# Differences of the normalised rows made inside the third gate/up, in the rows' own buffer, and projection steps begun two blocks later

## The chip, the cores and the metric

The kernel runs on one core of a Trainium2 chip. The metric is the device time of one execution in microseconds (us); lower is better. Of the core's engines the text calls TensorE PE (its weight loads PEld), VectorE DVE, ScalarE ACT, GpSimd POOL and SyncE SP. SP issues the DMA transfers.

## What is computed

The reference, cut to what matters:

```python
xn = layernorm(x)                                  # x: 2048 rows x 512
q  = (xn @ wq) in 32 heads of 128
p  = softmax(q @ k_cache^T * 128**-0.5)            # 2048 cached keys a head
s  = (p @ v_cache, heads side by side) @ wo
g  = silu((relu(xn @ W_gate) * (xn @ W_up)) @ W_down)   # inner width 1792
out = x + s * g
```

All inputs and the output are bf16. Two branches, attention and a gated MLP, read the same normalised rows xn.

## The kernel before, in words

**Layout.** The 2048 rows are four row blocks Q of 512 (QB = 4). x_sb holds the rows, xn_sb the normalised rows (16 tiles of 128 rows), and xnT their transposes, 128 x 4 x 2048: the model width in four chunks of 128, the rows along the free dimension. Rows are normalised on POOL (`ln_norm`) and transposed from xn_sb to xnT by DMA from SP's queue (L457). Nothing reads xn_sb after that.

**MLP stage.** For each Q, `emit_gate_up(Q)` makes 14 feature tiles fc. One tile is four gate and four up matmuls on PE (L539, L543), a relu on ACT (L498) and the product hT on DVE (L504). `emit_down(Q)` multiplies by W_down into ps_acc (L562), ACT takes a tanh (L570), DVE makes g_sb (L582). Q = 0 works on centred rows of its own; the other three on xnT. "Third gate/up" is Q = 2.

**The PSUM ring.** ps_r is a ring of three slots of two banks. `ring_acquire` makes PE wait for whatever last emptied the slot. Gate/up pairs, score pairs, projection steps and output tiles all take slots from it, in the order in which they are written.

**Attention stage.** There are 128 blocks b: head h = b // 4, row block Q = b % 4. A block is eight pairs p of key tiles. For a pair PE makes two score matmuls into a ring slot (`emit_S_tile`, L806), ACT takes the exponential into PT (L818), and three pairs later (LAG = 3) PE multiplies with V (`emit_PV_tile`, L915). When a block's last pair is done, DVE takes the reciprocal of the sums (L835), scales into Onorm (L838), and SP issues a DMA transpose into OT_store (L843).

**Queries.** Heads 0 and 1 are projected with four plain matmuls per head and row block (`emit_qp`, L645), evicted by a DVE cast (L652). From head 2 on, two heads (a pair pr) share a scheme of seven products in place of eight: `emit_st(pr, c, step)` with c = 0, 1 and step = 0 to 3. Steps 0 to 2 are two products of two matmuls each, step 3 one product (L717); DVE combines the results into QT_sb through cu and cv (L722, L729). The products need sums over xnT, TX (four arrays of 128 x 2 x 1024, fp16), made once on DVE by `emit_tx` (L667 to L672), and sums over the weights, SW, made per pair on POOL by `emit_sw` (L681 to L694). Step 0 does not read TX; step 1 is the first that does and waits for its token on PE.

**The output.** `emit_oproj_tile` multiplies a finished group g of four heads by W_o for one row tile n (L761) and adds to s_acc on DVE. For n = 0 it waits for all transposes of the group (`t_toks`). `emit_final_tile` does the last group (L949).

**The order around the change** is written out by hand. After the last gate/up come the projections of head 0, three score pairs, the last `emit_down`, then `emit_tx` on DVE's queue and `emit_sw(1)` on POOL's, then the loop over pairs. A `plan` says which extra items PE does in block b at pair p (always in one visit `emit_M`, which takes one ring slot): in blocks 0 and 1 at pair 4 the projections of head 1; in blocks 0 to 119 at pair 0 one step, eight steps a pair; from block 17 to 123 one output tile a block, at pair 4, or in the visit of step 3, or at pair 0 where there is no step. In block 2 of each eight SP issues the load of the weights of the pair after next (L271) and POOL's sums of it are written. `SB_` buffers live in a stack that is closed after the MLP stage, and the buffers of attention (SW, s_acc, OT_store, Onorm, cu, cv and, before, TX) are laid over it.

Of the kernel before, what the change touches and what calls it, by code (L numbers as in the profile page):

```python
# [30 lines left out]
def _wait(eng, tok):  # L31
    if tok is None:
        return
    sem, val = tok
    if val <= 0:
        return
    eng.wait_ge(sem.h, val)


def _wait_all(eng, toks):  # L40
    best = {}
    for t in toks:
        if t is None:
            continue
        sem, val = t
        k = id(sem)
        if k not in best or best[k][1] < val:
            best[k] = (sem, val)
    for sem, val in best.values():
        _wait(eng, (sem, val))  # L50


def bass_recurrent_scan__mha_block_cached__glu_gated_reglu__prompt_kernel(
# [56 lines left out]
    with ExitStack() as es:  # L110
        _cnt = [0]

        def S_(shape, dt, name):
            _cnt[0] += 1
            return es.enter_context(nc.sbuf_tensor(f"{name}_{_cnt[0]}", shape, dt))
# [20 lines left out]
        Wq_sb = [S_([128, DC, 2, Dh], BF16, "Wq_sb") for _ in range(2)]  # L136
        Wo_sb = [S_([128, G, D], BF16, "Wo_sb") for _ in range(2)]
        PT = [S_([128, 2, NQ], BF16, "PT") for _ in range(NPB)]
        es_b = ExitStack()

        def SB_(shape, dt, name):
            _cnt[0] += 1
            return es_b.enter_context(nc.sbuf_tensor(f"{name}_{_cnt[0]}", shape, dt))

        xn_sb = SB_([128, NT, D], BF16, "xn_sb")
        xc_sb = SB_([128, 4, D], BF16, "xc_sb")
        xcT = SB_([128, DC, NQ], BF16, "xcT")
        r2 = SB_([128, 4, 1], F32, "r2")
# [312 lines left out]
        def ln_task(i):  # L461
# [12 lines left out]
            elif i == 4 * (QB - 1) + 1:  # L474
# [4 lines left out]
                ln_hold["r2"] = sem_ln3.sig(  # L479
                    dve.tensor_scalar(r2h[:], r2[:], 0.5, None, op0=ALU.mult))  # L480

        gr_free = [None] * NSLOT
        y_bank_free = [None, None]
        sig_free = [None, None]
# [30 lines left out]
        def emit_gate_up(Q):  # L515
            qs = slice(Q * NQ, (Q + 1) * NQ)
            h_tok = None
            for fc in range(FC):
                fs = slice(fc * 128, (fc + 1) * 128)
                if Q == 0 and fc < HFC:  # L520
                    s = half_slots[fc]
                    finish_gate_up(Q, fc, s, half_tok[(fc, 0)], half_tok[(fc, 1)])
                    continue
                if Q == 0 and fc == HFC:
                    s = None
                    _wait_all(pe, acc_free)
                else:
                    s = ring_acquire()
                g_ps, u_ps = gu_banks(s)
                if fc == 0:  # L530
                    _wait_all(pe, xt_ready[Q])
                xT, xs = (xcT, slice(0, NQ)) if Q == 0 else (xnT, qs)
                if Q == 0 and fc in FCS:
                    k = FCS.index(fc)
                    pe.wait_ge(sem_wg[k].h, 16)
                    pe.wait_ge(sem_wu[k].h, 16)
                ins = None
                for c in range(DC):
                    ins = pe.matmul(g_ps, Wg_sb[:, c, fs], xT[:, c, xs],  # L539
                                    start=(c == 0), stop=(c == DC - 1))  # L540
                gtok = sem_gate.sig(ins)
                for c in range(DC):
                    ins = pe.matmul(u_ps, Wu_sb[:, c, fs], xT[:, c, xs],  # L543
                                    start=(c == 0), stop=(c == DC - 1))
                gu_tok = sem_gu.sig(ins)
                h_tok = finish_gate_up(Q, fc, s, gtok, gu_tok)
            return h_tok

        def emit_down(Q, h_last_tok):
# [50 lines left out]
        Onorm = [S_([128, 4, Dh], BF16, "Onorm") for _ in range(NON)]  # L600
        OT_store = [S_([128, G, S], BF16, "OT_store") for _ in range(2)]
        fin_tmp = [S_([128, D], BF16, "fin_tmp") for _ in range(4)]
        TX = S_([128, 4, DC // 2, S // 2], F16, "TX")
        SW = [S_([128, 4, DC // 2, Dh], F16, "SW") for _ in range(2)]
        cu = S_([128, NQ], F32, "cu")
        cv = S_([128, NQ], F32, "cv")
# [46 lines left out]
            qt_ready[(h, Q)] = etok  # L653
            return etok

        HS = S // 2
        HC = DC // 2
        tx_tok = []
        sw_tok = {}

        def emit_tx():
            b11 = xnT[:, 0:HC, 0:HS]
            b12 = xnT[:, 0:HC, HS:S]
            b21 = xnT[:, HC:DC, 0:HS]
            b22 = xnT[:, HC:DC, HS:S]
            _wait_all(dve, [t for Q in range(QB) for t in xt_ready[Q]])
            t1 = sem_T.sig(dve.tensor_tensor(TX[:, 0], b12, b11, ALU.subtract))  # L667
            sem_T.sig(dve.tensor_tensor(TX[:, 2], b22, b12, ALU.subtract))  # L668
            _wait(dve, t1)
            t2 = sem_T.sig(dve.tensor_tensor(TX[:, 1], b22, TX[:, 0], ALU.subtract))  # L670
            _wait(dve, t2)
            tx_tok.append(sem_T.sig(dve.tensor_tensor(TX[:, 3], TX[:, 1], b21, ALU.subtract)))  # L672

        def emit_sw(pr):
            b = pr % 2
# [22 lines left out]
        def emit_st(pr, c, step, *banks):  # L698
# [33 lines left out]
            if step == 1:  # L732
                if c == 0:
                    _wait(pe, sw_tok[(pr, 1)])
                    _wait(pe, tx_tok[0])
                p6 = prod(6, banks[0])
                p5 = prod(5, banks[1])
                st_tok["u"] = comb(cu[:], cu[:], banks[0], waits=(p6, st_tok["u"]))
                st_tok["v"] = comb(cv[:], cu[:], banks[1], waits=(p5, st_tok["u"]))
                return [st_tok["v"]]  # L740
# [241 lines left out]
        def at(b, p, *items):  # L982
            plan.setdefault((b, p), []).append(list(items))

        at(0, 4, (emit_qp, 1, 1, 0), (emit_qp, 1, 1, 1))
        at(1, 4, (emit_qp, 1, 1, 2), (emit_qp, 1, 1, 3))
        GB = G * QB
        LB = NBLK - QB
        tiles = {}
# [8 lines left out]
                        at(LB + k // 4, 4 * (k // 2 % 2))  # L998
                    plan[(LB + k // 4, 4 * (k // 2 % 2))][-1].append((emit_oproj_tile, 1, g, n))
        for b in range(LB):  # L1000
            pr, r = b // 8 + 1, b % 8
            c, step = r // 4, r % 4
            t = tiles.pop(b, None)
            if pr < NPR:
                if step < 3:
                    at(b, 0, (emit_st, 2, pr, c, step))
                else:
                    at(b, 0, (emit_st, 1, pr, c, step), *([t] if t else []))
                    t = None
            if t:  # L1010
                at(b, 4 if pr < NPR else 0, t)
        assert not tiles
        for Q in range(QB - 2):
            for j in range(4):
# [10 lines left out]
            emit_S_tile(gp, 1)  # L1025
        emit_down(QB - 1, hlast)
        glu_done_tok = sem_g.cur()
        _wait(dve, glu_done_tok)
        emit_tx()
        emit_sw(1)  # L1030

        for gp in range(LAG, TOTP):
            gq = gp - LAG
            bq, hq, Qq, pq = blk_of(gq)
            items = plan.pop((bq, pq), None)
            b, h, Q, p = blk_of(gp)
            if p == 0 and Q == 0:
                sp_head_start(h)
            open_S_pair(gp)
            emit_S_tile(gp, 0)  # L1040
            if pq == 0 and bq % 8 == 2:
                pr = bq // 8 + 2
                if pr < NPR:
                    _wait(sp, qp_done_tok[pr - 2])
                    issue_wq(pr)
                    emit_sw(pr)
            if items:
                emit_S_tile(gp, 1)
                for it in items:
                    emit_M(it)  # L1050
            emit_PV_tile(gq, 0)
            if not items:
                emit_S_tile(gp, 1)
            emit_PV_tile(gq, 1)
# [42 lines left out]
```

## Time and profile before

| what | before |
|---|---|
| time, median of 3 runs (lowest to highest) | 1280.52 us (1280.49 to 1281.59) |
| the profiled execution, its own time | 1280.7 us |
| its span, first to last instruction | 1279.4 us |
| mean granted PE clock over the span | 0.997 |
| HBM read, written | 32.77 MB, 2.10 MB |
| share of the 16 DMA engines in the main queue (q1) | 27.8% |
| score exponentials (ACT L818) | 1024, 960.9 us busy |
| PV matmuls (PE L915) | 8192, 764.3 us busy |

The profile is of one execution. Its rows give, for an engine and a line of the kernel, the number of instructions, the time in which at least one of them ran, the mean length of one, and the idle time of the engine just ahead of them with what ended it. Matmuls overlap in the pipeline, so the length of one is not what it adds to the time. "The chain that ended last" follows the work back from the last instruction to what released each step. The granted clock is the share of full speed that PE was allowed.

### The profile page before, as it was taken

Reading aid. Unit: us, or ns where it says so; the run is one execution under the profiler, and the core shown is the slowest. Engines: PE = TensorE matmul, PEld = TensorE weight load, DVE = VectorE, ACT = ScalarE, POOL = GpSimd, SP = SyncE. Lnnn points to the kernel's source line nnn. Section 1 sums busy time; section 2 is a strip of 40 time slices with the busy share of each in tenths; the row PEclk is TensorE's granted clock in tenths of the full one; section 3 lists DMA queues with packets and bytes.
Section 4 is the critical chain, followed back from the end, with each engine's and each line's share of the span. In section 5 each row is a group of like instructions: output and inputs, shape, how many; then the busy total and the mean of one; then the engine's idle time right before and its main releaser. Section 6 shows DMA issues by size and latency. Waiting matters only on the chain.

```text
span 1279.4 us, 26927 instructions
## 1 busy us (share of the span) xinstructions
PE 1257.1 (98%) x11740; PEld 828.7 (65%) x11965; DVE 458.8 (36%) x807; ACT 1011.1 (79%) x1112; POOL 97.5 (8%) x100
## 2 busy tenths in 40 slices
PE   9999989999999999999999999999999999999998
PEld 5444456666666666666666666666666666666665
DVE  7433342222332332333333333333333333335455
ACT  3322369998888888888888888888888888888985
POOL 2200020100001010101010010101010101000000
PEclk9999989999999999999999999999999999999999
DMA  9700002323322232322132332332231222232212
GB/s 268 153 1 1 1 18 51 59 50 59 50 50 55 67 59 47 59 49 57 35 58 47 75 51 46 59 67 55 50 59 34 59 47 54 51 67 47 50 18 75
DMA packets 233588, 72.14 MB, mean 56 GB/s; under 512 B 211200, under 2 KB 233472, under 8 KB 233472
## 3 DMA queue, kind: packets, MB, share of 16 engines
q1 hardware_dynamic: 232800, 70.02, 27.8%
q8 instruction: 95, 1.56, 0.5%
q10 hardware_dynamic: 672, 0.39, 0.1%
q14 instruction: 21, 0.17, 0.0%
HBM read 32.77 MB, written 2.10 MB: 27 GB/s over the span
## 4 chain that ended last, share of the span: by engine, by line
PE 86%; ACT 12%; issue 1%; DVE 1%; DVEq 0%
PE ps_acc L915 33%; PE ps_r L806 27%; ACT PT L818 12%; PE ps_r L761 7%; PE ps_r L717 6%; PE ps_acc L562 4%; PE ps_r L543 4%; PE ps_r L539 4%; PE ps_r L949 1%; PE ps_r L645 1%; PE ps_r L375 0%; DVE fin_tmp L957 0%; PE ps_r L441 0%; DVE TX L670 0%; DVE TX L668 0%
## 5 line engine op out<-in xcount | busy, mean ns | idle before, releaser
L818 ACT ACTIVATE PT<-ps_r 128x1024 bf16<-128x1024 f32 x1024 | 960.9, 1036 | 155.1 <-PE ps_r L806 145.3
L915 PE MATMUL ps_acc<-V_sb,PT 128*128 128x129 bf16 x8192 | 764.3, 220 | 9.9 <-ACT PT L818 0.9
L915 PEld LDWEIGHTS ps_acc<-V_sb,PT 128*128 128x128 bf16 x8192 | 612.8, 98 | 246.0 <-ACT PT L818 19.7
L806 PE MATMUL ps_r<-QT_sb,KT_sb 128*128 128x512 bf16 x1849 | 672.3, 380 | 6.2 <-DVE QT_sb L722 5.2
L806 PEld LDWEIGHTS ps_r<-QT_sb,KT_sb 128*128 128x128 bf16 x2048 | 191.9, 98 | 6.5 <-DVE QT_sb L722 5.4
L835 DVE RECIPROCAL rz_sb<-ps_acc 128x4 f32<-128x4 f32 x127 | 23.2, 183 | 445.7 <-PE ps_acc L915 445.7
L774 DVE TENSOR_TENSOR s_acc<-s_acc,ps_r 128x512 f32<-128x512 f32 x96 | 66.0, 688 | 214.4 <-PE ps_r L761 211.4
L761 PE MATMUL ps_r<-Wo_sb,OT_store 128*128 128x512 bf16 x442 | 114.2, 379 | 0.5
L681 POOL TENSOR_SCALAR Wq_sb<-Wq_sb 128x1024 bf16<-128x1024 bf16 x15 | 41.6, 2771 | 856.7 <-DMA Wq_sb<-in_A_wq_dram 856.7
L838 DVE TENSOR_TENSOR Onorm<-ps_acc,rz_sb 128x512 bf16<-128x512 f32 x127 | 87.8, 692 | 4.4
L761 PEld LDWEIGHTS ps_r<-Wo_sb,OT_store 128*128 128x128 bf16 x448 | 43.8, 98 | 52.9 <-ACT PT L818 1.1
L498 ACT ACTIVATE gr_sb<-ps_r 128x512 bf16<-128x512 f32 x55 | 32.6, 596 | 51.0 <-PE ps_r L539 50.4
L504 DVE TENSOR_TENSOR hT<-gr_sb,ps_r 128x512 bf16<-128x512 bf16 x55 | 37.8, 687 | 46.8 <-PE ps_r L543 41.7
L717 PE MATMUL ps_r<-TX,SW 128*128 128x512 f16 x180 | 48.6, 379 | 0.5
L562 PE MATMUL ps_acc<-Wd_sb,hT 128*128 128x512 bf16 x219 | 48.7, 379 | 0.3
L543 PE MATMUL ps_r<-xnT,Wu_sb 128*128 128x512 bf16 x165 | 42.8, 379 | 0.2
L722 DVE TENSOR_TENSOR QT_sb<-cu,ps_r 128x512 bf16<-128x512 f32 x60 | 41.3, 688 | 4.3
L539 PE MATMUL ps_r<-xnT,Wg_sb 128*128 128x512 bf16 x165 | 42.6, 379 | 0.2
L722 DVE TENSOR_TENSOR cu<-cu,ps_r 128x512 f32<-128x512 f32 x60 | 41.3, 688 | 0.0
L562 PEld LDWEIGHTS ps_acc<-Wd_sb,hT 128*128 128x128 bf16 x224 | 21.9, 98 | 26.4
L722 DVE TENSOR_TENSOR QT_sb<-cv,ps_r 128x512 bf16<-128x512 f32 x60 | 38.3, 681 | 0.0
L717 PEld LDWEIGHTS ps_r<-TX,SW 128*128 128x128 f16 x180 | 17.6, 98 | 21.3 <-ACT PT L818 1.5
(85 smaller groups left out, 419.7 us busy)
## 6 DMA issues: line engine op xcount, KB each, us to landing
V_sb<-in_A_v_cache_dram SPq DMA_DIRECT2D x32, 512.0 KB, 4.2
Wq_sb<-in_A_wq_dram SPq DMA_DIRECT2D x16, 256.0 KB, 2.9
Wo_sb<-in_A_wo_dram SPq DMA_DIRECT2D x8, 512.0 KB, 3.6
OT_store<-Onorm SPq DMA_TRANSPOSE x127, 2.5
Wd_sb<-in_B_W_down_dram SPq DMA_DIRECT2D x1, 1792.0 KB, 14.1
x_sb<-in_A_x_dram SPq DMA_DIRECT2D x3, 512.0 KB, 8.5
out_dram<-x_sb SPq DMA_DIRECT2D x6, 256.0 KB, 2.1
Wg_sb<-in_B_W_gate_dram SPq DMA_DIRECT2D x1, 640.0 KB, 9.7
```

What stands on the lines that cost most here:

```text
L539: ins = pe.matmul(g_ps, Wg_sb[:, c, fs], xT[:, c, xs], start=(c == 0), stop=(c == DC - 1))
L543: ins = pe.matmul(u_ps, Wu_sb[:, c, fs], xT[:, c, xs], start=(c == 0), stop=(c == DC - 1))
L562: ins = pe.matmul(ps_acc[:, jb, 0:D], hT[par][:, fc, j * 128:(j + 1) * 128], Wd_sb[:, fc, :], start=(fc == 0), stop=(fc == FC - 1))
L681: k = sem_sw.sig(pool.tensor_scalar(wflat, wflat, WSC, None, op0=ALU.mult))
L717: ins = pe.matmul(ps_r[:, bank, :], L(i), R(i), start=(i == 0), stop=(i == HC - 1))
L722: return sem_qpe.sig(dve.tensor_tensor(dst, a, ps_r[:, bank, :], op))
L761: ins = pe.matmul(ps_r[:, bank, 0:D], OT_store[g % 2][:, hh, n * 128:(n + 1) * 128], Wo_sb[g % 2][:, hh, :], start=(hh == 0), stop=(hh == ...
L774: dve.tensor_tensor(s_acc[:, n, :], s_acc[:, n, :], ps_r[:, bank, 0:D], ALU.add)
L806: ins = pe.matmul(ps_r[:, 2 * s + tt, :], KT_sb[h % 2][:, t * 128:(t + 1) * 128], QT_sb[qt_slot[(h, Q)]][:], start=True, stop=True)
L818: act.activation(PT[pb][:], ps_r[:, 2 * s:2 * s + 2, :], ACTF.Exp, scale=scale if h < 2 else scale / WSC)
L838: dve.tensor_tensor(Onorm[ob][:], o_ap, rz_sb[:].to_broadcast([128, 4, Dh]), ALU.mult))
L915: ins = pe.matmul(o_ap, PT[pb][:, tt, j * 128:(j + 1) * 128], V_sb[vb][:, t, 0:VW], start=(t == 0 and j % 2 == 0), stop=(t == KT - 1 and j ...
```

## The change

`emit_tx` is moved from after the MLP stage into the third gate/up: it becomes `emit_tx(k)`, k = 0 to 7, each with one eighth of the work (one of four sums, half of the columns), and is called after the hT product of feature tiles 2 to 9. TX no longer has memory of its own; it is a view of xn_sb, which moves from the MLP's stack to the kernel's outer one. The first piece waits for all transposes into xnT, since they read xn_sb. The projections of head 1 move from pair 4 to pair 0 of blocks 0 and 1. The steps begin in block 2 in place of block 0, and so end in block 121 in place of 119; tiles that share a visit with step 3 change with them. The load of the next weights and POOL's sums move from block 2 of each eight to block 4.

```diff
+        xn_sb = S_([128, NT, D], BF16, "xn_sb")
+        TX = xn_sb[:].bitcast(F16).rearrange("p n d -> p (n d)").rearrange(
+            "p (i c s) -> p i c s", i=4, c=DC // 2)
         es_b = ExitStack()
...
-        xn_sb = SB_([128, NT, D], BF16, "xn_sb")
...
+        def emit_tx(k):
+            c, i = divmod(k, 4)
+            lo = slice(c * NQ, (c + 1) * NQ)
+            hi = slice(HS + c * NQ, HS + (c + 1) * NQ)
+            b11, b12 = xnT[:, 0:HC, lo], xnT[:, 0:HC, hi]
+            b21, b22 = xnT[:, HC:DC, lo], xnT[:, HC:DC, hi]
+            X = [TX[:, j, :, lo] for j in range(4)]
+            if k == 0:
+                _wait_all(dve, [t for Q in range(QB) for t in xt_ready[Q]])
+            if i == 0:
+                t = dve.tensor_tensor(X[0], b12, b11, ALU.subtract)
+            elif i == 1:
+                t = dve.tensor_tensor(X[2], b22, b12, ALU.subtract)
+            elif i == 2:
+                _wait(dve, tx_tok[(c, 0)])
+                t = dve.tensor_tensor(X[1], b22, X[0], ALU.subtract)
+            else:
+                _wait(dve, tx_tok[(c, 2)])
+                t = dve.tensor_tensor(X[3], X[1], b21, ALU.subtract)
+            tx_tok[(c, i)] = sem_T.sig(t)
...
                 h_tok = finish_gate_up(Q, fc, s, gtok, gu_tok)
+                if Q == QB - 2 and 2 <= fc < 10:
+                    emit_tx(fc - 2)
...
-        TX = S_([128, 4, DC // 2, S // 2], F16, "TX")
...
-                    _wait(pe, tx_tok[0])
+                    _wait(pe, tx_tok[(1, 3)])
...
-        at(0, 4, (emit_qp, 1, 1, 0), (emit_qp, 1, 1, 1))
-        at(1, 4, (emit_qp, 1, 1, 2), (emit_qp, 1, 1, 3))
+        at(0, 0, (emit_qp, 1, 1, 0), (emit_qp, 1, 1, 1))
+        at(1, 0, (emit_qp, 1, 1, 2), (emit_qp, 1, 1, 3))
...
-            pr, r = b // 8 + 1, b % 8
+            pr, r = (b - 2) // 8 + 1, (b - 2) % 8
...
-            if pr < NPR:
+            if 0 < pr < NPR:
...
-                at(b, 4 if pr < NPR else 0, t)
+                at(b, 4 if 0 < pr < NPR else 0, t)
...
         glu_done_tok = sem_g.cur()
-        _wait(dve, glu_done_tok)
-        emit_tx()
         emit_sw(1)
...
-            if pq == 0 and bq % 8 == 2:
+            if pq == 0 and bq % 8 == 4:
```

The old `emit_tx` did the same four subtractions over 2 x 1024 columns each, in one piece a sum.

More of the change, by code (lines that the diff above doesn't have):

```diff
@@ L480, in ln_task @@
                     dve.tensor_scalar(r2h[:], r2[:], 0.5, None, op0=ALU.mult))
+        HS = S // 2
+        HC = DC // 2
+        tx_tok = {}
+        def emit_tx(k):
[18 more added lines that the diff above has]
+            tx_tok[(c, i)] = sem_T.sig(t)
         gr_free = [None] * NSLOT
@@ L654, in emit_qp @@
             return etok
-        HS = S // 2
-        HC = DC // 2
-        tx_tok = []
         sw_tok = {}
[L661 to L672, printed above, removed]
         def emit_sw(pr):
```

## The prediction

> **What bounds the kernel now.** I read the page's busy line and its chain first.
>
> ```profile
> PE 1257.1 (98%) x11740; PEld 828.7 (65%) x11965; DVE 458.8 (36%) x807; ACT 1011.1 (79%) x1112; POOL 97.5 (8%) x100
> PE 86%; ACT 12%; issue 1%; DVE 1%; DVEq 0%
> ```
>
> PE is busy for 98% of the span and is 86% of the chain that ended last, so the time is PE's work plus PE's pauses. The list of waits, longest total first, is the place to look for pauses; this row is the only one of a PE matmul over 1 us:
>
> ```profile
> PE ps_r L806 <- DVE QT_sb L722: 5.2, 1, 5.2
> ```
>
> One pause of 5.2 us, once. The timeline shows it where attention begins (columns: start, length, engine, line, operation, count, and in brackets the idle time before it and what ended it).
>
> ```profile
> 156.74 0.59 PE L806 MATMUL ps_r<-QT_sb,KT_sb 128*128 128x512 bf16 x2
> ...
> 157.17 1.03 PE L717 MATMUL ps_r<-xnT,Wq_sb 128*128 128x512 bf16 x4
> ...
> 157.57 0.69 DVE L582 SCALAR_TENSOR_TENSOR g_sb<-sig_sb,ps_acc 128x512 bf16<-128x512 f32 x1 [2.33 <-ACT sig_sb L570]
> ...
> 158.29 1.22 DVE L667 TENSOR_TENSOR TX<-xnT 128x2048 f16<-128x2048 bf16 x1
> ...
> 158.41 1.63 POOL L689 TENSOR_TENSOR SW<-Wq_sb 128x256 f16<-128x256 bf16 x1 [107.11 <-DVE g_sb L582]
> ...
> 159.43 1.69 DVE L668 TENSOR_TENSOR TX<-xnT 128x2048 f16<-128x2048 bf16 x1
> ...
> 161.04 1.68 DVE L670 TENSOR_TENSOR TX<-xnT,TX 128x2048 f16<-128x2048 bf16 x1
> ...
> 162.76 1.57 DVE L672 TENSOR_TENSOR TX<-TX,xnT 128x2048 f16<-128x2048 f16 x1
> ...
> 164.26 0.68 DVE L729 COPY cu<-ps_r 128x512 f32<-128x512 f32 x1
> ...
> 165.04 0.69 DVE L722 TENSOR_TENSOR QT_sb<-cu,ps_r 128x512 bf16<-128x512 f32 x1
> 165.78 0.61 PE L806 MATMUL ps_r<-QT_sb,KT_sb 128*128 128x512 bf16 x1 [5.19 <-DVE QT_sb L722]
> ```
>
> PE does the four matmuls of projection step 0 (L717) into a slot of the three-slot ring. DVE cannot empty that slot: the four TX sums are queued in front of its two evictions (L729, L722), from 158.29 to 164.3. Two score pairs later PE needs the slot again and stands still for 5.19 us. The windows show what that costs beyond the pause (columns: window, length, busy time and count of PE, PEld, DVE, ACT, POOL, granted clock, DMA):
>
> ```profile
> 156.74:160.60 3.86, 3.80 (x34) 2.32 (x33) 3.00 (x3) 2.59 (x4) 2.19 (x2) 1.00 0.00 2
> 160.60:165.78 5.18, 0.00 (x0) 0.00 (x0) 4.99 (x5) 0.86 (x1) 4.19 (x3) 0.73 0.00 0
> 165.78:169.80 4.02, 4.01 (x16) 2.05 (x17) 0.00 (x0) 2.05 (x2) 0.00 (x0) 0.50 0.01 4
> 169.80:173.89 4.09, 4.04 (x44) 2.79 (x43) 1.38 (x2) 1.80 (x2) 0.00 (x0) 1.00 0.00 0
> 173.89:183.56 9.67, 9.62 (x94) 6.34 (x94) 3.59 (x6) 7.54 (x9) 0.00 (x0) 1.00 0.07 15
> ```
>
> After the pause PE runs 4.02 us at a granted clock of 0.50, so about 2.0 us more are lost. The pause costs some 7.2 us in all.
>
> **Block times.** Attention is 128 blocks, and each closes with one reciprocal (L835), so the distance between two of them is a block's time:
>
> ```profile
> 174.09 0.18 DVE L835 RECIPROCAL rz_sb<-ps_acc 128x4 f32<-128x4 f32 x1 [2.42 <-PE ps_acc L915]
> 183.76 0.18 DVE L835 RECIPROCAL rz_sb<-ps_acc 128x4 f32<-128x4 f32 x1 [2.42 <-PE ps_acc L915]
> 191.70 0.18 DVE L835 RECIPROCAL rz_sb<-ps_acc 128x4 f32<-128x4 f32 x1 [5.20 <-PE ps_acc L915]
> 199.60 0.18 DVE L835 RECIPROCAL rz_sb<-ps_acc 128x4 f32<-128x4 f32 x1 [6.35 <-PE ps_acc L915]
> ...
> 302.74 0.18 DVE L835 RECIPROCAL rz_sb<-ps_acc 128x4 f32<-128x4 f32 x1 [5.57 <-PE ps_acc L915]
> 311.54 0.18 DVE L835 RECIPROCAL rz_sb<-ps_acc 128x4 f32<-128x4 f32 x1 [2.42 <-PE ps_acc L915]
> 320.35 0.18 DVE L835 RECIPROCAL rz_sb<-ps_acc 128x4 f32<-128x4 f32 x1 [2.42 <-PE ps_acc L915]
> 328.72 0.18 DVE L835 RECIPROCAL rz_sb<-ps_acc 128x4 f32<-128x4 f32 x1 [5.96 <-PE ps_acc L915]
> ...
> 1198.60 0.18 DVE L835 RECIPROCAL rz_sb<-ps_acc 128x4 f32<-128x4 f32 x1 [4.51 <-PE ps_acc L915]
> ...
> 1230.37 0.18 DVE L835 RECIPROCAL rz_sb<-ps_acc 128x4 f32<-128x4 f32 x1 [4.51 <-PE ps_acc L915]
> ```
>
> They close blocks 0, 1, 2, 3, 16, 17, 18, 19, 119 and 123. Hence: block 1 (step of four matmuls, and eight matmuls of L645) 9.67; a block with a four-matmul step alone 7.94; with step 3 alone (two matmuls) 7.90; step and output tile 8.81; step 3 and tile in one visit 8.38; tile alone 7.94 (31.77 for four). Four matmuls are worth 0.87, since PE sets the pace; only step 3 alone is held at 7.90 by ACT. Block 0 begins with the pair at 156.74, as block 1 does at 173.89: 17.15 us.
>
> **The change part by part.** *TX sums to the third gate/up.* Eight pieces of 1024 elements a partition take the place of four of 2048, one behind each of the hT products of feature tiles 2 to 9:
>
> ```profile
> 119.29 0.69 DVE L504 TENSOR_TENSOR hT<-gr_sb,ps_r 128x512 bf16<-128x512 bf16 x1 [1.04 <-PE ps_r L543]
> ...
> 121.01 0.69 DVE L504 TENSOR_TENSOR hT<-gr_sb,ps_r 128x512 bf16<-128x512 bf16 x1 [1.04 <-PE ps_r L543]
> ```
>
> ```profile
> L774 DVE TENSOR_TENSOR s_acc<-s_acc,ps_r 128x512 f32<-128x512 f32 x96 | 66.0, 688 | 214.4 <-PE ps_r L761 211.4 <-remote 0.4
> ...
> L973 DVE TENSOR_TENSOR x_sb<-x_sb,fin_tmp 128x512 bf16<-128x512 bf16 x16 | 6.6, 416 | 0.0
> ```
>
> ```profile
> 103.76:156.50 52.74, 0.00 (x0) 1.00 0.00 1
> ```
>
> (The last is the window for POOL alone: idle throughout.) DVE has 1.04 us free per tile of 1.72. No row has a piece. From 416 ns for 512 two-byte SBUF elements (L973) and 1224 for 2048 (L667), a line gives 416 + 512 x 808/1536 = 685 ns. Lower end: half of 1224, 612. Upper end: two operations of 688 as on unpacked data (L774), 1376. I take 685, whose rows have the same kind of operands; the slower TX sums of 1.57 to 1.69 ran beside POOL, which is idle here, and half of 1.69 would fit too. 0.69 + 0.69 = 1.38 is under 1.72, so PE waits for nothing: cost 0, at the upper end 8 x (0.69 + 1.38 - 1.72) = 2.8 us. The pieces' own waits are for sums one or two tiles old. The wait of the first is for the last transposes into xnT, issued long before:
>
> ```profile
> 46.10 5.41 SPq L457 DMA_TRANSPOSE xnT<-xn_sb  x4
> ```
>
> DVE's in-order queue is thus not held, nor hT behind it.
>
> *Block 0* gets the eight matmuls of L645 (0.87 x 2) at its start in place of step 0. Behind the last g_sb (157.57 + 0.69 = 158.26) DVE has only two casts. The matmuls end near 157.17 + 1.73 = 158.9, the second cast near 159.8; the slot is needed two pairs (2 x 0.88) after 158.9, at 160.7. So the slot is free 0.9 us early; what is late next is again PE itself. Block 0 becomes 7.94 + 0.87 = 8.81 in place of 17.15: -8.34. *Block 1* loses its step: 8.81 in place of 9.67: -0.86. I take 8.81 from the blocks with eight extra matmuls in two visits; here they stand in one visit. Lower end 8.75; upper end 9.2, since ACT held the block of step 3 alone 0.4 above its matmuls.
>
> *Steps two blocks later.* Blocks 2 to 16 keep one step each, with three blocks of step 3 in place of four: +0.04. Blocks 17 to 119 keep 26 visits of step 3 with a tile: 0. Block 120 gains step 2 (7.94 to 8.81, +0.87), block 121 step 3 in the tile's visit (7.94 to 8.38, +0.44). Queries are still made at least two blocks before use (h2's second in block 6, opened at the end of block 8). The Wq load moves from block 2 of eight to block 4:
>
> ```profile
> Wq_sb<-in_A_wq_dram SPq DMA_DIRECT2D x16, 256.0 KB, 2.9
> ```
>
> It stands on SP behind the K and V loads of a head's start and waits for a projection three blocks old; POOL's sums follow it. Their user is six blocks later as before, over 47 us, so I cost load and sums at 0; if that cover were gone, a late load would hold step 0 once per eight blocks.
>
> **Sum**: -8.34 - 0.86 + 0.04 + 0.87 + 0.44 = -7.85 us. The profiled execution took 1280.7 (span 1279.4), 0.2 over the median 1280.52 of the three runs: 1280.7 - 7.85 = 1272.85, on the median's scale 1272.7.
>
> **Rivals.**
>
> *The sums set the pace of the third gate/up* (6%). Against: 1.04 us free and the rows of packed sums. For: each operand is two runs of 512, a form that no row has. At the upper end +2.8: 1275.5.
>
> *The half clock stays* (5%): the clock falls at the handover for another reason than PE's pause, and only the pause goes. Of the 7.85, 2.0 return: 1274.7. Against: the clock is 1.00 until 160.60 and falls inside the pause. [...]
>
> *The change does not do what it says* (4%): block 0 stalls as long as now because the reused slot waits for something other than TX, such as casts later than 160.7. Then block 0 stays at 17.15 and the rest is -0.86 + 1.35 = +0.49: 1281.0, no difference. Against: DVE's queue at 158.26 is empty but for the casts.
>
> *Slower* (3%): the first output tile of each of seven groups moves from the middle to the start of blocks 17, 33, ... 113, and PE waits there for the group's last transposes.
>
> ```profile
> 295.73 9.13 SPq L843 DMA_TRANSPOSE OT_store<-Onorm  x2
> ...
> 302.97 1.03 PE L717 MATMUL ps_r<-TX,SW 128*128 128x512 f16 x4
> ```
>
> ```profile
> DMA to landing us min/median/max: 2.4/2.5/5.1
> ```
>
> The transpose of block 15 is issued at 295.73 and lands by 300.8 at the worst of 127; the visit in block 17 begins at 302.97 and step 3 takes 0.43 of it: 2.6 us of cover. Past that, each us costs seven. The whole gain is lost when landings come 2.6 + 7.85/7 = 3.7 us later than the worst seen; at 5 us later, 7 x 2.4 = 16.8: 1289.5.
>
> **How the numbers follow.** Forecast 1272.7, 82%, with a range of its own of 1271.5 to 1274.3 (one-visit blocks from -0.06 to +0.4 each, the pieces, and some 0.5 between runs). The range 1271.3 to 1275.5 reaches to the half clock and the upper end of the sums; it leaves out 7% for the two last rivals and as much for errors of size. A difference under 0.2%, 2.6 us, can hardly be told from none. Faster: 82 + 6 + 5 = 93%. Same: 4%. Slower: 3%.
>
> **What would show it.** Right: no PE wait near 160, a granted clock of 1.00 through the first blocks; reciprocals of blocks 0 and 1 near 165.7 and 174.6; eight TX pieces of about 0.69 with hT still 1.72 apart; blocks 120 and 121 at 8.81 and 8.38. Wrong: hT further apart in the third gate/up; a PE wait for a cast in block 0; a wait on OT_store at the first tile of a group; blocks 0 and 1 well over 8.81.

## The result and the profile after

The changed kernel takes 1274.39 us, median of 4 runs (1274.05 to 1274.78); the kernel before took 1280.51 beside it (1280.43 to 1281.59). The ratio is 0.995, with a 95% interval of 0.9933 to 0.9968. That is 6.12 us less, where the prediction had 7.85. The profiled execution after took 1274.78 (span 1273.5).

The busy line and the chain that ended last, from the page of after:

```profile
PE 1265.6 (99%) x11965; PEld 827.5 (65%) x11965; DVE 457.4 (36%) x811; ACT 1010.8 (79%) x1112; POOL 93.6 (7%) x100
PE 97%; ACT 2%; DVE 0%; DMA 0%; issue 0%; SPq 0%
```

PE's share of the chain reads 97% in place of 86%, but that does not measure the change: the trace of before holds 11740 of the 11965 matmuls, and on the page of e_pad (below: the kernel before with eight empty instructions), whose trace holds all of them, the share is 96% with the same pause of 5.2 us. DVE has 811 instructions in place of 807: eight pieces for four sums. Keep that 4 in mind. The longest waits of PE in after:

```profile
PE ps_r L377 <- PEq L1092: 0.8, 1, 0.8
PE ps_acc L927 <- ACT PT L830: 0.7, 3, 0.2
```

The row of 5.2 us is gone and none of 1 us has come. The timeline of after at the same place:

```profile
157.50 0.59 PE L818 MATMUL ps_r<-QT_sb,KT_sb 128*128 128x512 bf16 x2
...
157.93 1.89 PE L673 MATMUL ps_r<-xnT,Wq_sb 128*128 128x512 bf16 x8
...
158.33 0.69 DVE L611 SCALAR_TENSOR_TENSOR g_sb<-sig_sb,ps_acc 128x512 bf16<-128x512 f32 x1 [2.33 <-ACT sig_sb L599]
...
158.99 0.69 DVE L680 CAST QT_sb<-ps_r 128x512 bf16<-128x512 f32 x1
...
159.86 0.69 DVE L680 CAST QT_sb<-ps_r 128x512 bf16<-128x512 f32 x1 [0.17 <-PE ps_r L673]
...
161.44 0.38 PE L818 MATMUL ps_r<-QT_sb,KT_sb 128*128 128x512 bf16 x1
...
166.30 0.59 PE L818 MATMUL ps_r<-QT_sb,KT_sb 128*128 128x512 bf16 x2
```

Behind g_sb come only the two casts. The slot is free at 160.55 and PE's score pair at 161.44 carries no bracket: it waited for nothing. The pair at 166.30 opens block 1. The windows of after, over the handover, over the rest of block 0, and over the third gate/up:

```profile
157.50:161.30 3.80, 3.80 (x32) 2.27 (x31) 2.05 (x3) 1.84 (x3) 2.05 (x4) 1.00 0.00 0
161.30:166.30 5.00, 5.00 (x60) 3.71 (x59) 0.00 (x0) 5.00 (x6) 0.54 (x1) 1.00 0.02 3
78.00:106.00 28.00, 28.00 (x131) 12.68 (x130) 15.75 (x24) 8.96 (x15) 0.00 (x0) 1.00 0.00 1
```

PE is busy in every microsecond of all three, at a granted clock of 1.00. DVE's 15.75 us in the third gate/up were 10.32 before (15 operations then, 24 now), and PE does not feel it.

The closes of blocks 0, 1 and 2, and of 119, 120 and 121:

```profile
166.51 0.18 DVE L847 RECIPROCAL rz_sb<-ps_acc 128x4 f32<-128x4 f32 x1 [5.96 <-PE ps_acc L927]
175.31 0.18 DVE L847 RECIPROCAL rz_sb<-ps_acc 128x4 f32<-128x4 f32 x1 [5.96 <-PE ps_acc L927]
183.26 0.18 DVE L847 RECIPROCAL rz_sb<-ps_acc 128x4 f32<-128x4 f32 x1 [5.60 <-PE ps_acc L927]
...
1190.19 0.18 DVE L847 RECIPROCAL rz_sb<-ps_acc 128x4 f32<-128x4 f32 x1 [0.97 <-PE ps_acc L927]
1199.00 0.18 DVE L847 RECIPROCAL rz_sb<-ps_acc 128x4 f32<-128x4 f32 x1 [0.97 <-PE ps_acc L927]
1207.37 0.18 DVE L847 RECIPROCAL rz_sb<-ps_acc 128x4 f32<-128x4 f32 x1 [4.51 <-PE ps_acc L927]
```

Block 0 took 166.30 - 157.50 = 8.80 us from its score pair to that of block 1, block 1 8.80, block 2 7.95, block 120 8.81, block 121 8.37. The blocks gave all that was forecast of them, and yet the span is 5.9 us shorter (1279.4 to 1273.5) and not 7.85. Two places took the rest back. One is the start, shown by the first hT product of before and then of after:

```profile
10.54 0.69 DVE L504 TENSOR_TENSOR hT<-gr_sb,ps_r 128x512 bf16<-128x512 bf16 x1 [2.39 <-PE ps_r L441]
```

```profile
11.30 0.69 DVE L531 TENSOR_TENSOR hT<-gr_sb,ps_r 128x512 bf16<-128x512 bf16 x1 [2.39 <-PE ps_r L443]
```

In this execution of after everything up to attention is 0.76 us late, because a load of x landed later (DVE's statistics of the third row tile start at 6.41 in place of 5.64, 0.49 of it a wait for the load). The other is the end, shown by the last reciprocal in before and then in after, each with SP's wait for the last store of the output behind it (total us, times, longest us):

```profile
1259.46 0.18 DVE L835 RECIPROCAL rz_sb<-ps_acc 128x4 f32<-128x4 f32 x1 [2.01 <-PE ps_acc L915]
```

```profile
SPq L1068 <- DMA out_dram<-x_sb: 1.4, 1, 1.4
```

```profile
1252.36 0.18 DVE L847 RECIPROCAL rz_sb<-ps_acc 128x4 f32<-128x4 f32 x1 [2.02 <-PE ps_acc L927]
```

```profile
SPq L1078 <- DMA out_dram<-x_sb: 2.5, 1, 2.5
```

From that reciprocal to the end of the span it is 1273.5 - 1252.36 = 21.1 us, in before 1279.4 - 1259.46 = 19.9; nearly all of the 1.2 us more is the wait for the last store (2.5 in place of 1.4). In all, -7.85 + 0.76 + 1.2 = -5.9.

### The profile page after: what moved, and what is told of

It reads as the page before. It is cut to its first block, busy times and chain, and to the rows that moved or that the text cites. A ratio compares the mean times of both kernels' runs of the same rounds, so it can differ in the third digit from the quotient of the medians.

```text
span 1273.5 us, 27150 instructions
## 1 busy us (share of the span) xinstructions
PE 1265.6 (99%) x11965; PEld 827.5 (65%) x11965; DVE 457.4 (36%) x811; ACT 1010.8 (79%) x1112; POOL 93.6 (7%) x100
## 3 DMA queue, kind: packets, MB, share of 16 engines
q8 instruction: 95, 1.56, 0.5%
## 4 chain that ended last, share of the span: by engine, by line
PE 97%; ACT 2%; DVE 0%; DMA 0%; issue 0%; SPq 0%
PE ps_acc L927 36%; PE ps_r L818 34%; PE ps_r L773 8%; PE ps_r L729 7%; PE ps_acc L591 4%; PE ps_r L566 4%; PE ps_r L570 4%; ACT PT L830 2%; PE ps_r L961 1%; PE ps_r L673 1%; DMA x_sb<-in_A_x_dram 0%; DVE fin_tmp L969 0%; PE ps_r L443 0%; DVE x_sb L985 0%; PE ps_acc L570 0%
## 5 line engine op out<-in xcount | busy, mean ns | idle before, releaser
L818 PE MATMUL ps_r<-QT_sb,KT_sb 128*128 128x512 bf16 x2048 | 741.4, 379 | 0.0
L729 PE MATMUL ps_r<-xn_sb,SW 128*128 128x512 f16 x180 | 48.6, 379 | 0.0
L729 PEld LDWEIGHTS ps_r<-xn_sb,SW 128*128 128x128 f16 x180 | 17.6, 98 | 21.3 <-ACT PT L830 1.8
```

Source lines behind the costliest of these rows:

```text
L729: ins = pe.matmul(ps_r[:, bank, :], L(i), R(i), start=(i == 0), stop=(i == HC - 1))
L818: ins = pe.matmul(ps_r[:, 2 * s + tt, :], KT_sb[h % 2][:, t * 128:(t + 1) * 128], QT_sb[qt_slot[(h, Q)]][:], start=True, stop=True)
```

## The experiments

Open were: whether the gain is that of the sums alone, whether the sums cost DVE anything, what the half clock has to do with it, and whether the late start and the late store belong to the change. Times are medians, in brackets the lowest and highest and the number of runs; each ratio is to the kernel before, run on the same chip, with its 95% interval. The kernel before took 1280.87 (21 runs) beside c_after, e_tx_only, e_plan_only and e_two_late, 1281.00 (14 runs) beside e_double, e_four, e_pad and e_best, and 1280.79 (15 runs) beside e_pad4, e_after_pad4, e_best2 and e_triple.

**c_after**: the changed kernel again, unaltered.

> The changed kernel once more, unaltered, as a control for the 1.7 us between the sum of -7.85 us and the -6.1 us of the medians. In its first trace the blocks moved as summed, but the first gate/up began 0.76 us later than in the trace of before (first loads of x and the weights landed later) and the last store landed 1.2 us later. Theory A (these two are chance of one execution): in this trace at least one of the two is back near before's value, and the blocks are the same to 0.1 us. Theory B (they belong to the changed kernel): the first gate/up late by 0.7 to 0.8 us and the last store landing about 3 us after its issue again. Time 1273 to 1275 us in both.

1274.22 (1274.02 to 1275.12, 5), ratio 0.9947 [0.9934, 0.9961]: 6.65 us less. The first hT starts at 10.84 here, 0.46 earlier than in the trace above; SP's wait for the last store is long again, 2.4 us. The late start is chance of an execution (over all traces of the experiments the first hT lies between 10.71 and 11.33, and the trace of before, 10.54, is the earliest). The late store comes back: it belongs to the kernel.

**e_tx_only**: the sums moved, the plan of before.

```diff
-        at(0, 0, (emit_qp, 1, 1, 0), (emit_qp, 1, 1, 1))
-        at(1, 0, (emit_qp, 1, 1, 2), (emit_qp, 1, 1, 3))
+        at(0, 4, (emit_qp, 1, 1, 0), (emit_qp, 1, 1, 1))
+        at(1, 4, (emit_qp, 1, 1, 2), (emit_qp, 1, 1, 3))
...
-            pr, r = (b - 2) // 8 + 1, (b - 2) % 8
+            pr, r = b // 8 + 1, b % 8
...
+        _wait(dve, glu_done_tok)
         emit_sw(1)
...
-            if pq == 0 and bq % 8 == 4:
+            if pq == 0 and bq % 8 == 2:
```

> The sums alone are moved into the third gate/up; the plan is that of before (steps from block 0, head 1's projections at pair 4, weights loaded in block 2 of eight). Theory A (the pause of 5.2 us and the half clock behind it are the gain, the plan is worth only 0.37): block 0 falls from 17.15 to about 9.7 us, all others stay, the blocks' sum is -7.48, the clock is 1.00; time 0.2 to 0.6 us over the changed kernel's. Rival (the later steps are needed to take the pause away, since step 1 of block 1 now waits for POOL's sums): a PE wait at block 1 and 2 us or more over the changed kernel.

1274.60 (1274.49 to 1274.65, 5), ratio 0.9949 [0.9936, 0.9961]. No PE wait reaches 1 us and the clock is 1.00. Blocks 0 and 1, by their closes:

```profile
166.95 0.18 DVE L847 RECIPROCAL rz_sb<-ps_acc 128x4 f32<-128x4 f32 x1 [2.42 <-PE ps_acc L927]
176.62 0.18 DVE L847 RECIPROCAL rz_sb<-ps_acc 128x4 f32<-128x4 f32 x1 [2.42 <-PE ps_acc L927]
```

Block 1 is at 9.67, as before the change. So 6.27 of the 6.65 us are the sums', and the plan adds 0.38. The prediction's terms give the same split: with step 0 left in it, block 0 is 9.67 in place of 8.81, +0.86, against the +0.49 that the plan costs from block 1 on; 0.37.

**e_plan_only**: the kernel before with the new plan, the four sums where they were.

```diff
-        at(0, 4, (emit_qp, 1, 1, 0), (emit_qp, 1, 1, 1))
+        at(0, 0, (emit_qp, 1, 1, 0), (emit_qp, 1, 1, 1))
...
-            pr, r = b // 8 + 1, b % 8
+            pr, r = (b - 2) // 8 + 1, (b - 2) % 8
...
-            if pq == 0 and bq % 8 == 2:
+            if pq == 0 and bq % 8 == 4:
```

> The plan alone is changed; the four TX sums stay between the last g_sb and the first evictions on DVE. Theory A: the casts of head 1's projections now stand behind the sums, so PE pauses in block 0 as before, until about 165.8 us, and the half clock follows; block 0 about 16.3, the blocks' sum -0.4 us against before: no difference that can be told. Rival (deferring the step is what frees the slot): no PE wait in block 0 and most of the 6 us gained.

1279.30 (1279.06 to 1280.71, 11), ratio 0.9988 [0.9979, 0.9997]. Wait, timeline and window:

```profile
PE ps_r L806 <- DVE QT_sb L652: 4.3, 1, 4.3
```

```profile
164.72 1.27 DVE L652 CAST QT_sb<-ps_r 128x512 bf16<-128x512 f32 x2
166.05 0.61 PE L806 MATMUL ps_r<-QT_sb,KT_sb 128*128 128x512 bf16 x1 [4.31 <-DVE QT_sb L652]
```

```profile
165.50:169.10 3.60, 3.05 (x17) 1.95 (x18) 0.49 (x1) 1.02 (x1) 0.00 (x0) 0.53 0.02 5
```

The pause stays, now for the projections' casts: whatever PE puts into the ring first is held while the sums stand on DVE. It is 0.9 shorter, since the eight matmuls put ahead of it are work that PE does before it stops; what I expected of this run had left that out, and so the run is 1.57 us faster than before where I had expected no difference that can be told. The half clock stays too: by the mean of 0.53 over these 3.60 us it lasts an estimated 3.4 us (3.6 x 0.47 / 0.5), if the clock is at 0.50 or at 1.00. The runs fall into two groups: 1279.06 to 1279.34 with a mean clock of 0.999, and 1279.82 to 1280.71 with 0.997.

**e_two_late**: e_tx_only, but two of the four sums (four of the eight pieces) stay at the handover, to make a pause of middle length.

```diff
-                if Q == QB - 2 and 2 <= fc < 10:
+                if Q == QB - 2 and 2 <= fc < 10 and (fc - 2) % 4 < 2:
                     emit_tx(fc - 2)
...
         glu_done_tok = sem_g.cur()
+        for k in (2, 6, 3, 7):
+            emit_tx(k)
         emit_sw(1)
```

> Plan of before; of the four sums two are made in the third gate/up and two (X1 and X3, in four pieces) stay at the handover. DVE then needs about 3.2 us in place of 6.0 in front of the evictions, and PE's pause shrinks from 5.2 to about 2.4 us. Theory A (the clock halves only in a pause long enough): granted clock 1.00 afterwards, block 0 about 12.3 us, the blocks' sum about -4.8 against before. Rival (any pause here halves the clock, or the handover does): clock 0.50 for some us after the pause, block 0 about 13.3 to 14.3, sum -2.9 to -3.9.

1279.36 (1277.72 to 1280.71, 11), ratio 0.9985 [0.9977, 0.9994]. Timeline and window of its traced execution, which took 1277.93:

```profile
163.81 0.39 PE L818 MATMUL ps_r<-QT_sb,KT_sb 128*128 128x512 bf16 x1 [2.94 <-DVE QT_sb L734]
```

```profile
164.00:172.00 8.00, 8.00 (x75) 5.11 (x74) 3.08 (x6) 5.71 (x6) 0.00 (x0) 1.00 0.01 2
```

A pause of 2.94 us, and the full clock behind it. (I had expected a pause of 2.4; three of the four pieces ran beside POOL's sums and took 1.15 to 1.16 us, where a piece alone takes 0.68.) But only 3 of the 11 runs are like that one (1277.72 to 1277.93); the other 8 take 1279.25 to 1280.71, most with a mean clock of 0.998 in place of 0.999. From the median of the three (1277.76) to that of the eight (1279.42) it is 1.7 us, by an estimate what 3.4 us at a clock of 0.50 cost. So the pause is the main cost, and at the handover the half clock was seen only with a pause (5.2 us in before, 4.3 in e_plan_only; 1.00 without one in after and e_tx_only); if the half clock is what parts the two groups, at this length it comes in most executions (8 of 11) and not in all.

**e_double**: each piece made twice, the second time into memory that nothing reads.

```diff
+        dup_sb = SB_([128, 2, DC // 2, NQ], F16, "dup_sb")
...
+            D2 = dup_sb[:, k % 2]
+            _wait(dve, dup_tok.get(k - 2))
+            p, q = [(b12, b11), (b22, b12), (b22, X[0]), (X[1], b21)][i]
+            dup_tok[k] = sem_T.sig(dve.tensor_tensor(D2, p, q, ALU.subtract))
```

> The changed kernel with each of the eight pieces made twice, the second time into a scratch buffer that nothing reads: DVE then has 0.69 + 2 x 0.685 = 2.06 us of work per feature tile of 1.73. Theory A (PE waits for an hT product only three ring slots later, so DVE may fall behind by some 2.6 us before PE notices, and it falls behind by 8 x 0.34 = 2.7): the third gate/up grows by 0.1 to 0.3 us, time within 0.3 us of the changed kernel's 1274.2 to 1274.4. Rival, as the prediction priced its upper end (DVE's excess lands on PE at once): +2.7 us, 1277.

1273.06 (1273.00 to 1273.22, 5), ratio 0.9938 [0.9924, 0.9952]. The window of the third gate/up:

```profile
78.00:106.00 28.00, 28.00 (x131) 12.73 (x130) 19.48 (x32) 8.96 (x15) 0.00 (x0) 1.00 0.00 1
```

Eight more operations, and PE is still busy throughout: the sums are hidden with room to spare. More: it is 1.2 us faster than c_after, which does without the extra work, and its last store is prompt (1.4 us). The number of instructions alone doesn't make the store late.

**e_four**: the four whole sums of before, behind feature tiles 2, 4, 6 and 8.

```diff
...
-                if Q == QB - 2 and 2 <= fc < 10:
-                    emit_tx(fc - 2)
+                if Q == QB - 2 and fc in (2, 4, 6, 8):
+                    emit_tx(fc // 2 - 1)
```

> The changed kernel with four whole sums of 2048 elements behind feature tiles 2, 4, 6 and 8 in place of eight pieces, so DVE has four instructions fewer (1209 in the trace, as before, in place of 1213). Traces with 1213 show one more 8 KB transfer in the instruction queue (q14), 1.4 us ahead of the end, and the last store lands 1.1 us later than in traces with 1209. Theory A (that fetch, set off by the longer instruction stream of DVE, delays the last store): the fetch and the delay are gone, from the last reciprocal to the end 19.9 us in place of 21.0, time about 1273.1; DVE needs 1.91 us for a tile with a sum, the next tile gives it back, so nothing is lost in the third gate/up. Rival (the tail comes with the place of xn_sb or of the buffers behind it): tail 21.0 again, time 1274.2 to 1274.4.

(The 1209 and 1213 count every DVE record of the trace. The 807 and 811 of the page leave out those for registers, branches and semaphores.)

1273.12 (1273.06 to 1273.66, 5), ratio 0.9940 [0.9926, 0.9954]: 7.88 us less than before, the forecast sum. SP's wait, then the first of the sums:

```profile
SPq L1074 <- DMA out_dram<-x_sb: 1.4, 1, 1.4
```

```profile
85.66 1.22 DVE L494 TENSOR_TENSOR xn_sb<-xnT 128x2048 f16<-128x2048 bf16 x1
86.80 0.68 DVE L527 TENSOR_TENSOR hT<-gr_sb,ps_r 128x512 bf16<-128x512 bf16 x1
```

The sum takes 1.22 us and the next hT follows it with no bracket, late by a little, and PE does not wait. With DVE back at 807 instructions the store is prompt, and the queue that carries instructions makes 21 transfers, as before the change. On the page of after it makes one more:

```profile
q14 instruction: 22, 0.18, 0.1%
```

**e_pad**: the kernel before with eight empty instructions on DVE (one-column memsets that nothing reads), in blocks 4 to 11.

```diff
...
+            if pq == 4 and 4 <= bq < 12:
+                dve.memset(pad_sb[:, bq - 4:bq - 3], 0.0)
```

> The kernel before with eight added memsets of one column on DVE in the middle of blocks 4 to 11, where DVE is idle; nothing reads what they write. Theory A (the length of DVE's instruction stream decides the extra fetch): one more 8 KB transfer in q14 near the end, from the last reciprocal to the end 21.0 us in place of 19.9, time about 1.1 us over before. Rival (the tail comes with the place of xn_sb): 19.9 us, time as before.

1281.43 (1280.66 to 1281.91, 11), ratio 1.0003 [0.9994, 1.0012]. The theory that one more instruction transfer makes the store late falls in this form: the page counts 22 of them, and the wait is 1.4 us. The DMA view of the half microsecond in which the 22nd falls:

```profile
q1 hardware_dynamic: 140, 0.13, 77.9%
q14 instruction: 1, 0.01, 8.4%
```

Here (1276.7 to 1277.2) it runs while the stores' data still stream, 3.2 us ahead of the end. In after it comes at 1272.07, 1.38 ahead of the end. The view of 1272.0 to 1272.3, and then of 1272.3 to 1272.7:

```profile
q14 instruction: 1, 0.01, 6.4%
```

```profile
DMA packets 1, 0.00 MB, mean 0 GB/s; under 512 B 1, under 2 KB 1, under 8 KB 1
```

The data of the store are through by 1272.0. Then the one packet of 8 KB of instructions takes 307 ns (6.4% of 16 engines in 0.30 us), and behind it follows one lone packet, under 512 B, of the queue that carries the stores. That leaves the theory that the moment decides: the fetch must fall into the end of the last store. The next two kernels try it with four instructions, the number that the change adds.

**e_pad4**: the kernel before with four empty instructions. **e_after_pad4**: the same four in the changed kernel.

```diff
...
+            if pq == 4 and 4 <= bq < 8:
+                dve.memset(pad_sb[:, bq - 4:bq - 3], 0.0)
```

> The kernel before with four (in place of eight) added memsets of one column on DVE, in blocks 4 to 7: 1213 DVE instructions, the number of the changed kernel. With eight more the extra 8 KB fetch came 3.2 us ahead of the end and the last store was not late; with twelve more (e_double) 4.2 us ahead, not late either; with four more it came 1.4 us ahead, in the flight of the last store. Theory A (what counts is when the fetch falls): here it falls about 1.4 us ahead of the end, the last store lands some 1.1 us later, 21.0 us from the last reciprocal to the end. Rival (the late store comes with the place of xn_sb, not with the fetch): 19.9 us, although the fetch is there.

> The changed kernel with four added memsets on DVE: 1217 instructions. Theory A (when the fetch falls): the fetch comes earlier than the last store, about 3 us ahead of the end; from the last reciprocal to the end 19.9 us, and the kernel with more instructions is the faster one, about 1273.1. Rival (place of xn_sb, or number of instructions): 21.0 us, 1274.3.

e_pad4: 1282.35 (1281.61 to 1283.11, 11), ratio 1.0010 [1.0001, 1.0019]. e_after_pad4: 1273.07 (1273.02 to 1273.37, 5), ratio 0.9939 [0.9926, 0.9951]. SP's wait in e_pad4, and in e_after_pad4:

```profile
SPq L1071 <- DMA out_dram<-x_sb: 2.5, 1, 2.5
```

```profile
SPq L1081 <- DMA out_dram<-x_sb: 1.4, 1, 1.4
```

Four instructions that do nothing make the old kernel's last store 1.1 us late, and four more make the new kernel's prompt and the kernel 1.15 us faster than c_after. In e_pad4 the fetch falls 1.4 us ahead of the end (at 1279.09 of 1280.5), in e_after_pad4 3.3 (at 1268.44 of 1271.7). (By its own median e_pad4 is 1.56 us above before; the interval reaches from 0.1 to 2.4.) That is the term that the prediction lacked.

**e_best**: e_four, with half of head 1's projections for block 1 moved to pair 4 of block 5.

```diff
-        at(1, 0, (emit_qp, 1, 1, 2), (emit_qp, 1, 1, 3))
+        at(1, 0, (emit_qp, 1, 1, 2))
+        at(5, 4, (emit_qp, 1, 1, 3))
...
-            if pq == 0 and bq % 8 == 4:
+            if pq == 0 and bq % 8 == 6:
```

> Four whole sums as in e_four; besides, the projection of head 1's last row block moves from block 1 to pair 4 of block 5, whose step 3 alone leaves PE waiting for ACT, and the next weights are loaded in block 6 of eight. Theory A (only blocks with step 3 alone have PE time to spare, 0.40 us each): block 1 falls from 8.81 to 7.94 and block 5 rises from 7.90 to 8.37, another -0.4 us on e_four, about 1272.7. Rival (the two matmuls' worth of slack isn't there in block 5): 8.8 in block 5 and no gain on e_four.

1273.09 (1272.98 to 1273.53, 5), ratio 0.9939 [0.9926, 0.9952]: nothing over e_four. Block 1 falls to 7.94 (166.06 to 174.00), but block 5 pays. The timeline with the closes of blocks 4 and 5:

```profile
197.83 0.18 DVE L843 RECIPROCAL rz_sb<-ps_acc 128x4 f32<-128x4 f32 x1 [5.20 <-PE ps_acc L923]
...
198.89 0.61 PE L923 MATMUL ps_acc<-V_sb,PT 128*128 128x129 bf16 x8 [0.23 <-ACT PT L826]
...
206.60 0.18 DVE L843 RECIPROCAL rz_sb<-ps_acc 128x4 f32<-128x4 f32 x1 [2.42 <-PE ps_acc L923]
```

It takes 8.77. Step 3 is in it with its two matmuls; beside it PE waits for ACT (0.23 here, as three times in the list of after, whose blocks of step 3 alone are three), and the four matmuls at pair 4 come on top with their full 0.87.

**e_best2**: the same, but these four matmuls in the visit of step 3.

```diff
-        at(5, 4, (emit_qp, 1, 1, 3))
...
-            t = tiles.pop(b, None)
+            t = tiles.pop(b, None) if b != 5 else (emit_qp, 1, 1, 3)
```

> As e_best, but the projection of head 1's last row block shares the visit of step 3 in block 5 in place of a visit of its own (there block 5 came to 8.77). Theory A (a visit takes one of three ring slots and PE then waits for ACT, so a visit costs some 0.83 us however little is in it; the slack can be used in the same visit only): block 5 at 8.38, block 1 at 7.94, 0.4 us under e_four, about 1272.7. Rival (block 5 is held by something else, ACT's eight exponentials for instance): 8.77 again and 1273.1.

1272.72 (1272.66 to 1273.24, 5), ratio 0.9935 [0.9922, 0.9949]. The closes of blocks 1, 4 and 5:

```profile
174.48 0.18 DVE L843 RECIPROCAL rz_sb<-ps_acc 128x4 f32<-128x4 f32 x1 [5.96 <-PE ps_acc L923]
...
198.31 0.18 DVE L843 RECIPROCAL rz_sb<-ps_acc 128x4 f32<-128x4 f32 x1 [5.20 <-PE ps_acc L923]
...
206.68 0.18 DVE L843 RECIPROCAL rz_sb<-ps_acc 128x4 f32<-128x4 f32 x1 [5.96 <-PE ps_acc L923]
```

Block 1 is at 7.94 (from 166.54) and block 5 at 8.37: in one visit the four matmuls cost 0.47 beside step 3. This version has the lowest time of all: 8.07 us less than before, where c_after has 6.65 less.

**e_triple**: each piece three times, to look for the edge of the cover.

```diff
...
+            for m in range(2):
+                _wait(dve, dup_tok.get(m))
+                dup_tok[m] = sem_T.sig(dve.tensor_tensor(dup_sb[:, m], p, q, ALU.subtract))
```

> The changed kernel with each piece made three times (two copies into scratch that nothing reads): DVE has 2.74 us of work for a feature tile of 1.73. Theory A (three ring slots let DVE fall behind by 2.6 us, beyond that PE waits): it falls 8 x 1.02 = 8.1 us behind, PE waits 5 to 6 us in the third gate/up, time about 1278 to 1279, and DVE's excess over the slack, not its whole, is what PE loses. Rival 1 (PE loses the whole excess): 8 us, 1281. Rival 2 (nothing is lost, the products catch up before the down matmuls need them): 1273.

1276.05 (1276.03 to 1276.11, 5), ratio 0.9961 [0.9949, 0.9974]. PE's wait and the hT products of two tiles in a row:

```profile
PE ps_r L572 <- DVE hT L537: 2.3, 4, 0.7
```

```profile
87.43 0.68 DVE L537 TENSOR_TENSOR hT<-gr_sb,ps_r 128x512 bf16<-128x512 bf16 x1
...
89.83 0.68 DVE L537 TENSOR_TENSOR hT<-gr_sb,ps_r 128x512 bf16<-128x512 bf16 x1
```

Now the sums do set the pace: hT is 2.40 us apart in place of 1.73, and the kernel takes 1276.05 us where e_double takes 1273.06: 3.0 lost, where I had expected 5 to 6.

## Why the prediction was right, and what it missed

**The number.** The measured 1274.39 lies inside the stated range (1271.3 to 1275.5), but 1.7 us above the forecast of 1272.7 and just above the range that the prediction gave its main case (to 1274.3).

**The bound and the pause: right.** The pause came from the sums in front of the evictions. With the sums moved it is gone, with two of them left it is 2.94 us, with the plan alone moved it is 4.3.

**Block times: right.** Block 0 8.80 (forecast 8.81), block 1 8.80 (8.81), block 120 8.81 (8.81), block 121 8.37 (8.38). The clean measure of the sum is e_four, whose last store is as prompt as that of before: -7.88, forecast -7.85. That they agree to 0.03 is luck, since what the half clock costs the kernel before differs between executions by more (see below).

**The pieces: right, with wrong rows.** They take 684 ns (forecast 685), by the first of their groups in after:

```profile
L498 DVE TENSOR_TENSOR xn_sb<-xnT x2: 684/684/684, 86.1 to 93.0; 128x1024 f16<-128x1024 bf16 x2
```

So the two runs of 512 in an operand cost nothing over the line drawn between the rows of 512 and 2048; one run of 1024 was not measured. The choice of the faster row was right too: with POOL idle the whole sums of e_four take 1.22 us each, and the 1.57 to 1.69 of before belong to sums beside POOL's, which themselves took 1.53 to 1.64 us there and 0.67 alone. But the rows that I quoted for DVE's free time (119 to 121 us, and POOL idle from 103.76) are of the fourth gate/up; the third runs from about 80 to 104 us. Its own row in before has the same gap, so the number held by luck of a regular loop:

```profile
84.75 0.69 DVE L504 TENSOR_TENSOR hT<-gr_sb,ps_r 128x512 bf16<-128x512 bf16 x1 [1.04 <-PE ps_r L543]
```

**The upper end of the first rival: too dear.** I priced 8 x (0.69 + 1.38 - 1.72) = 2.8 us for pieces of double length. e_double puts just that load on DVE and costs nothing. Two things were left out. The three slots of the ring let DVE fall behind before PE stands, and operations of 0.69 us start 0.60 apart, as the timeline of after shows:

```profile
85.52 0.69 DVE L531 TENSOR_TENSOR hT<-gr_sb,ps_r 128x512 bf16<-128x512 bf16 x1 [1.04 <-PE ps_r L570]
86.12 0.68 DVE L498 TENSOR_TENSOR xn_sb<-xnT 128x1024 f16<-128x1024 bf16 x1
```

Two pieces and an hT so take 3 x 0.60 = 1.80 a tile, 8 x (1.80 - 1.73) = 0.6 us too much in all, which the slots take up. e_triple shows how much they take: 8 x (2.40 - 1.73) = 5.4 us of excess, of which 3.0 was paid, so about 2.4.

**The half clock: right that it goes with the pause.** In before the mean granted clock is 1.00 from 160.60 to 162.90, 0.78 from there to 163.00, 0.50 from 163.00 to 169.70, 0.73 to 169.85 and 1.00 behind that. So it fell some 2.4 us into the pause and stayed at 0.50 for 6.8 us, 2.8 of them in the pause and 4.0 behind it; in e_plan_only, behind a pause of 4.3, it is an estimated 3.4. In after, without the pause, the clock is 1.00 throughout 157.50 to 175.10. The kernel whose pause is 2.94 us long took 1.3 us or more longer in 8 of 11 runs than in the other three. That those 8 owe it to the clock is read from their times and mean clocks alone; the one profile of this kernel is of an execution at full clock. How long a pause must be for the clock to fall, and why one execution is caught and another not, no run shows.

The cost behind the pause, 2.0 us in the prediction, is that of one execution. Of the 50 runs of the kernel before beside the experiments, 28 have a mean clock of 0.997 and a median of 1281.28 us, 22 have 0.998 and 1280.48: an estimated 0.8 us between executions.

**The rivals fell.** The half clock did not stay: the measured 1274.39 is near the 1274.7 of that rival, but the clock is 1.00 at the handover, and the missing time is at the two ends of the span. The change does what it says. The output tiles that move wait for nothing: the row of transposes into OT_store in after is

```profile
DMA to landing us min/median/max: 2.4/2.5/5.3
```

and PE has no wait for OT_store in its list.

**The step that failed is the sum**: it took the time outside the blocks as unchanged. "Eight pieces take the place of four" was costed by its durations alone, 8 x 0.69, all hidden. With the four more instructions comes one more transfer of the queue that carries instructions (21 with 807 instructions of DVE on the page of before, 22 with 811 on that of after), and this one now falls 1.38 us ahead of the end, behind the data of the last store and ahead of one last packet of its queue: the wait for it is 2.5 us in place of 1.4, and from the last reciprocal to the end it is +1.2 us. With it, the forecast is -7.85 + 1.2 = -6.65, and c_after has -6.65. That these agree to the hundredth is luck: the interval of c_after reaches from 5.0 to 8.5 us less. The rest, up to the -6.12 of the first comparison, is within the spread of start and clock between few runs.

## What to carry to other kernels

Look for the long pause of the engine that bounds the kernel, and ask what stands on the in-order queue of the engine that it waits for; work on that queue that depends on nothing recent can be done earlier, in a stage with gaps. (Here four sums stood on DVE's queue from 158.29 to 164.3 in front of two evictions, and PE paused 5.2 us.) Test how much of a gap there is by doing the hidden work twice: an e_double that costs nothing says more than any sum of durations. And at differences near 1 us look at both ends of the span before you explain the middle: four empty instructions moved the wait for the last store by 1.1 us in both directions here (2.5 in place of 1.4 in e_pad4, 1.4 in place of 2.5 in e_after_pad4).

## What the runs showed that I had not expected

- **The last store was late where an instruction transfer fell at its end.** In after and e_pad4 the views put an 8 KB instruction transfer 1.4 us ahead of the end, and the wait for the last store is 2.5 us in both. Where it begins 3.2 us ahead (e_pad), 3.3 (e_after_pad4) or before 1268.0, 3.9 or more ahead (e_double), the wait is 1.4, as in before, which makes one transfer fewer. In e_tx_only and e_two_late, which wait 2.4 and 2.5 us, and in e_triple, which waits 1.4, the view shows only that it begins after 1268.0, in the last 5.3, 8.6 and 6.8 us; for c_after, which waits 2.4, no view shows it. In after one lone packet of the store's queue stands behind the transfer. Whether the two wait for the same DMA engine the views do not show, and why the landing takes so much longer than the transfer (0.3 us in after) stays open.
- **A visit with two matmuls is paid almost like one with four.** Step 3 alone makes a block of 7.90 against 7.94 with four matmuls; put together with four others in one visit (e_best2) both cost 8.37, apart (e_best) 8.77.
- **DVE's operations overlap**: 0.69 us long, 0.60 from start to start in the third gate/up (85.52 and 86.12 in after).
